# Half of a depthwise convolution moved from TensorE to VectorE and ScalarE, with new scheduler durations and dummy matmuls, in a pooled-attention and gated feed-forward kernel

## Chip, cores, metric

One NeuronCore of a Trainium2 chip. The metric is the device time of one execution in microseconds, the median of a kernel's runs; the profile of an execution shows a span that is 1.7 to 2.4 us shorter than its time. Engines are named as in the profile: PE (TensorE), PEld (its weight loads), DVE (VectorE), ACT (ScalarE), POOL (GpSimd), SP (SyncE).

## The reference

```python
# q, k, v: (8, 8, 576, 64) fp32;  w_in (512, 1024), conv_w (3, 1024), w_out (1024, 512)
k_p = k.reshape(B, H, 72, 8, D).mean(axis=3)              # pool k and v over 8 positions
v_p = v.reshape(B, H, 72, 8, D).mean(axis=3)
attn = softmax(q @ k_p.T / sqrt(D));  x = attn @ v_p      # x: (8, 576, 512) after the heads are joined
h = relu(x @ w_in)                                        # (8, 576, 1024)
conv_out[s] = conv_w[0] * h[s-1] + conv_w[1] * h[s] + conv_w[2] * h[s+1]   # per feature, zero padded
out = (h * sigmoid(conv_out)) @ w_out                     # (8, 576, 512)
```

The convolution has three taps for each feature. With features on partitions and positions along the free dimension it is either three matmuls with diagonal weights that accumulate in PSUM, or three multiplies by a per-partition scalar and two adds.

## The kernel before

The kernel writes each operation as a task with an estimated duration, the buffers it reads and writes, and a priority. A list scheduler (`Planner`) simulates the engines with these estimates and emits the instructions of each engine in that order. The estimates cost no time themselves: they decide the order, and every engine then works through its own list in that order.

```python
class Planner:
    N_PS = 4                 # PSUM slots, each a tile of [P, 2, 512] in fp32
    DMA_RATE = 220e3         # bytes per us that the planner assumes for loads
    DMA_LAT = 2.2
    SEM = 0.12
    LAT = {"PE": 0.20, "ACT": 0.16, "DVE": 0.10, "POOL": 0.12, ...}
    # ... order(): takes the operation that can start first, by priority, on the engine that ends it first

def conv(b, f, pr):                                   # batch b, block f of 128 features
    def fn(e):
        t = slot(key)
        for kk in range(3):
            for i in range(2):
                nc.tensor.matmul(out=t[:, i, 0:HC], lhsT=dw[:, f, kk, :],       # diagonal weights
                                 rhs=hT[m][:, f, 1 + kk + i * HC:1 + kk + (i + 1) * HC],
                                 start=(kk == 0), stop=(kk == 2))
    pl.add(f"conv.{b}.{f}", "PE", 0.73, fn, ...)
    # ScalarE: tg = tanh(conv / 2) from PSUM;  VectorE: tg += 1;  VectorE: gT = tg * hT
# ... mm1: h block (8 matmuls), relu on ScalarE into hT;  mm2: 128 rows of the output (8 matmuls of 512)
```

One batch runs through loads, sums over k and v (DVE), transposes (PE) with evacuations (ACT or DVE), scores (PE), exponentials (ACT), the product with v (PE), normalisation (DVE), transposes and copies, then `mm1`, the convolution, the gate and, for two batches at a time, `mm2`. The planner interleaves the attention of batch b+1 with the feed-forward of batch b.

The softmax here doesn't subtract the row's maximum and nothing guards it: scores larger than these inputs give would overflow.

## Time and profile before

| | before |
|---|---|
| time, median of 3 runs first (262.15 to 262.91) | 262.34 us |
| span of the profiled run | 259.9 us |
| busy: PE / DVE / ACT | 235.1 / 126.8 / 166.5 us |
| first product block of batch 0 starts | 23.3 us |
| first product block of batch 1 starts | 62.0 us |
| last product block ends | 244.2 us |

The last three rows are milestones in the trace that divide the run into a prologue (attention alone), the first batch's feed-forward with the hole in which batch 1's attention stands almost alone, a dense part with PE close to full, and a tail. The prediction below shows the lines that carry this.

### The profile page before, as it was taken

The page shows a single profiled execution, that of the slowest core. Times are in us where ns is not written, and L with a number is a line of the kernel's source. Part 1 is how long each engine was busy: PE and PEld are TensorE (multiplying, and loading weights), DVE is VectorE, ACT ScalarE, POOL GpSimd, SP SyncE. Part 2 cuts the span into 40 slices and gives each one's busy share as a digit, 9 for nine tenths or more (in the row PEclk, how much of TensorE's full clock was granted, in tenths as well). Part 3 has the DMA queues.
Part 4 walks back from the last instruction along what each step waited for, and adds up shares of the span by engine and source line. Part 5 has one row for each costly group of instructions (what it writes and reads, how often), then busy time and mean ns, then how long its engine had stood idle before and what let it go on. Part 6 is the DMA issues. An engine that isn't in the chain of part 4 may idle for free.

```text
span 259.9 us, 4786 instructions
## 1 busy us (share of the span) xinstructions
PE 235.1 (90%) x1985; PEld 166.9 (64%) x1985; DVE 126.8 (49%) x307; ACT 166.5 (64%) x271; POOL 25.6 (10%) x47
## 2 busy tenths in 40 slices
PE   0488997969999999999999999999999999999992
PEld 0356774458877767676757767686768767667540
DVE  2684346556587628923766427421753237123210
ACT  1574673657978857686658856596658855547521
POOL 8761001302102101210000000000000000000000
PEclk9995999968999999999999999999999999999999
DMA  7999997996854774894207002020102102102214
GB/s 180 204 199 208 207 205 113 195 201 114 130 89 83 105 127 112 143 171 108 82 0 171 23 21 83 0 83 32 49 6 78 43 0 83 57 25 83 81 40 161
DMA packets 20617, 26.60 MB, mean 102 GB/s; under 512 B 2396, under 2 KB 14516, under 8 KB 20596
## 3 DMA queue, kind: packets, MB, share of 16 engines
q0 software_dynamic: 15024, 15.67, 38.5%
q1 hardware_dynamic: 5572, 10.63, 11.8%
q8 instruction: 15, 0.25, 0.4%
q14 instruction: 6, 0.05, 0.1%
HBM read 32.52 MB, written 9.44 MB: 161 GB/s over the span
## 4 chain that ended last, share of the span: by engine, by line
PE 76%; ACT 13%; DVE 6%; DMA 3%; issue 1%; ACTq 0%; POOLq 0%
PE psf L478 24%; PE psf L531 23%; PE psf L497 18%; PE psf L402 5%; ACT tg L504 3%; DMA q_b<-in_q_dram 3%; ACT attnT L413 3%; DVE xx L443 2%; PE psb L385 2%; ACT osb L539 2%; PE psb L457 2%; PE psf L430 1%; ACT xT L463 1%; ACT qT L391 1%; ACT kTz L357 1%
## 5 line engine op out<-in xcount | busy, mean ns | idle before, releaser
L478 PE MATMUL psf<-xT,w_in 128*128 128x288 bf16 x512 | 74.4, 290 | 1.2 <-ACT xT L463 0.5
L531 PE MATMUL psf<-w_out,gT 128*128 128x512 bf16 x288 | 65.9, 379 | 1.4 <-DVE gT L514 1.1
L509 DVE TENSOR_SCALAR tg<-tg 128x576 bf16<-128x576 bf16 x64 | 20.1, 314 | 82.9 <-ACT tg L504 82.3
L478 PEld LDWEIGHTS <-w_in 128*128 128x128 bf16 x512 | 50.3, 99 | 15.7 <-issue 1.5
L497 PE MATMUL psf<-hT,dw 128*128 128x288 bf16 x384 | 57.9, 286 | 1.1 <-ACT kTz L357 1.0
L484 ACT ACTIVATE hT<-psf 128x576 bf16<-128x576 f32 x64 | 41.7, 652 | 18.0 <-PE psf L478 17.6
L531 PEld LDWEIGHTS <-gT 128*128 128x128 bf16 x288 | 27.9, 98 | 32.0 <-DVE gT L514 2.2
L504 ACT ACTIVATE tg<-psf 128x576 bf16<-128x576 f32 x64 | 41.5, 649 | 7.7 <-PE psf L497 2.4
L539 ACT COPY osb<-psf 128x1024 f32<-128x1024 f32 (+1 forms) x20 | 18.5, 927 | 42.3 <-PE psf L531 42.3
L497 PEld LDWEIGHTS <-dw 128*128 128x128 bf16 x384 | 37.1, 97 | 11.2 <-issue 1.8
L413 ACT ACTIVATE attnT<-psf 72x576 bf16<-72x576 f32 x64 | 39.7, 644 | 1.9 <-PE psf L402 1.9
L514 DVE TENSOR_TENSOR gT<-tg,hT 128x576 bf16<-128x576 bf16 x64 | 29.0, 453 | 1.5
L402 PE MATMUL psf<-qT,kTz 128*72 128x288 bf16 x128 | 26.0, 303 | 2.2 <-ACT qT L391 1.4
L443 DVE TENSOR_TENSOR xx<-psf,rr 128x512 bf16<-128x512 f32 x40 | 26.8, 684 | 0.4
L385 PE MATMUL psb<-ident,q_b 128*128 128x128 bf16 x144 | 12.9, 240 | 9.2 <-DMA q_b<-in_q_dram 8.5
L402 PEld LDWEIGHTS <-kTz 128*72 128x72 bf16 x128 | 15.4, 120 | 6.8 <-issue 1.6
L430 PE MATMUL psf<-vaug,attnT 72*128 72x65 bf16 x320 | 16.3, 198 | 2.5 <-ACT attnT L413 1.1
L391 ACT COPY qT<-psb 128x768 bf16<-128x768 bf16 x17 | 13.1, 805 | 8.5 <-PE psb L385 8.5
L457 PE MATMUL psb<-perm,xx 128*128 128x128 bf16 x160 | 16.9, 237 | 1.5 <-DVE xx L443 1.1
L430 PEld LDWEIGHTS <-attnT 72*128 72x128 bf16 x320 | 14.3, 101 | 5.2 <-ACT attnT L413 3.0
L463 ACT COPY xT<-psb 128x512 bf16<-128x512 bf16 (+1 forms) x25 | 13.2, 536 | 6.8 <-PE psb L457 6.6
L385 PEld LDWEIGHTS <-q_b 128*128 128x128 bf16 x144 | 10.6, 109 | 10.3 <-DMA q_b<-in_q_dram 8.6
(39 smaller groups left out, 115.5 us busy)
## 6 DMA issues: line engine op xcount, KB each, us to landing
out_dram<-osb SPq DMA_DIRECT2D x16, 512.0 KB, 2.8
v_b<-in_v_dram POOLq DMA_DIRECT2D x8, 576.0 KB, 11.3
k_b<-in_k_dram POOLq DMA_DIRECT2D x7, 576.0 KB, 7.6
q_b<-in_q_dram POOLq DMA_DIRECT2D x7, 576.0 KB, 6.4
k_f<-in_k_dram SPq DMA_DIRECT2D x2, 576.0 KB, 5.8
w_in<-in_moe_w_in_dram POOLq DMA_DIRECT2D x4, 256.0 KB, 10.2
w_out<-in_moe_w_out_dram POOLq DMA_DIRECT2D x2, 512.0 KB, 13.8
out_dram<-osb SPq DMA_DIRECT2D x4, 256.0 KB, 2.0
```

The source lines that it names most:

```text
L385: nc.tensor.transpose(out=t[:, 0, i * P:(i + 1) * P], in_=q_b[m][:, j:j + 2, :].rearrange("p i d -> p (i d)"), identity=ident)
L402: nc.tensor.matmul(out=t[0:Sp, par, 0:HC], lhsT=kTz[m][:, par, h * Sp:(h + 1) * Sp], rhs=qT[m][:, :, h * A:(h + 1) * A], start=True, stop= ...
L413: nc.scalar.activation(out=attnT[m][:, h, :].rearrange("p (c i x) -> p i c x", i=2, x=32), in_=slot(key)[0:Sp, :, 0:HC].rearrange("p i (c ...
L430: nc.tensor.matmul(out=a[:, h // 4, c:c + D + 1], lhsT=attnT[m][:, h, u0:u0 + 128], rhs=vaug[m][:, h, :], start=True, stop=True)
L443: nc.vector.tensor_tensor(out=xx[i3].rearrange("p (g h e) -> p g h e", g=2, h=4), in0=av_view()[:, :, :, 0:D], in1=rr[i3].rearrange("p (g ...
L478: nc.tensor.matmul(out=t[:, i, 0:HC], lhsT=w_in[:, c, f * P:(f + 1) * P], rhs=xT[m][:, c, i * HC:(i + 1) * HC], start=(c == 0), stop=(c == ...
L484: nc.scalar.activation(out=hT[m][:, f, 2:S + 2].rearrange("p (i x) -> p i x", i=2), in_=slot(key)[:, :, 0:HC], func=ACT.Relu, scale=0.5)
L497: nc.tensor.matmul(out=t[:, i, 0:HC], lhsT=dw[:, f, kk, :], rhs=hT[m][:, f, 1 + kk + i * HC:1 + kk + (i + 1) * HC], start=(kk == 0), stop= ...
L504: nc.scalar.activation(out=tg[i3].rearrange("p (i x) -> p i x", i=2), in_=slot(key)[:, :, 0:HC], func=ACT.Tanh, scale=0.5)
L514: nc.vector.tensor_tensor(out=gT[(b // 2) % 2][:, f, o:o + S], in0=tg[i3], in1=hT[m][:, f, 2:S + 2], op=OP.mult)
L531: nc.tensor.matmul(out=a[:, x, :], lhsT=g[:, c, t * P:(t + 1) * P], rhs=w_out[:, c, :], start=(c == 0), stop=(c == n_fb - 1))
L539: copy_on(e)(out=osb[i3][:, 0:n, :], in_=slot(key)[:, 0:n, :])
```

## The change

The intent: take work from PE, the bound. Convolution blocks 1, 3, 5 and 7 of each batch go to VectorE and ScalarE in bf16; the planner gets durations and latencies nearer to the trace, and a higher load rate; dummy matmuls on a zeroed tile fill planned PE gaps of the first 24 us, to keep the array's clock up; and each PSUM tile takes the slot that the planner gave it. Cut to its core:

```diff
-    DMA_RATE = 220e3
-    DMA_LAT = 2.2
-    SEM = 0.12
+    DMA_RATE = 330e3
+    DMA_LAT = 2.0
+    SEM = 0.05
+    WARM = 24.0
...
+            if e == "PE" and s < self.WARM and s - free.get(e, 0.0) > 0.3:
+                ...   # a free slot x:  self.gaps[i] = (s - f0, x)
...
+    def warm(gap, x):
+        t = pp.tile([P, 2, 512], FP32, name="psw", tag=f"ps{x}")
+        for _ in range(min(int((gap - 0.2) / 0.1), 60)):
+            nc.tensor.matmul(out=t[:, 0, 0:P], lhsT=zero[:, 0:P], rhs=zero[:, 0:P], start=True, stop=True)
...
+    OFF = [(1, 3, 5, 7) for b in range(B)]
...
+    def conv_off(b, f, pr):
+        for kk in (1, 0, 2):
+            def fn(e, kk=kk):
+                s = cw[:, kk * n_fb + f:kk * n_fb + f + 1]
+                src = hT[m][:, f, 1 + kk:1 + kk + S]
+                if e == "ACT":
+                    nc.scalar.activation(out=cv[y][:, kk, :], in_=src, func=ACT.Copy, scale=s)
+                else:
+                    nc.vector.tensor_scalar(out=cv[y][:, kk, :], in0=src, scalar1=s, scalar2=None, op0=OP.mult)
+            pl.add(f"cp{kk}.{b}.{f}", {"DVE": 0.225, "ACT": 0.59}, 0, fn, ...)
+        for kk in (0, 2):
+            def fn(e, kk=kk):
+                nc.vector.tensor_tensor(out=cv[y][:, 1, :], in0=cv[y][:, 1, :], in1=cv[y][:, kk, :], op=OP.add)
+            pl.add(f"ca{kk}.{b}.{f}", "DVE", 0.375, fn, ...)
+        # then tanh on ScalarE, from SBUF
...
-            pl.add(f"qTe.{b}.{g}", {"ACT": 0.73, "DVE": 0.95}, 0, fn, ...)
+            pl.add(f"qTe.{b}.{g}", {"ACT": 0.71, "DVE": 0.475}, 0, fn, ...)
         # ... some twenty other durations in the same way; kz on DVE 0.72 -> 0.375, xte on DVE 0.66 -> 0.345
```

More of the change, by code (lines that the diff above doesn't have):

```diff
@@ L61, in add @@
         return o.i
-    LAT = {"PE": 0.20, "ACT": 0.16, "DVE": 0.10, "POOL": 0.12, "SP": 0.0, "ACTQ": 0.0}
+    LAT = {"PE": 0.17, "ACT": 0.10, "DVE": 0.08, "POOL": 0.12, "SP": 0.0, "ACTQ": 0.0}
     def order(self):
@@ L73, in order @@
         free = {}
-        slots = [0.0] * self.N_PS
-        held = {}
+        slots = {i: 0.0 for i in range(self.N_PS)}
+        held = self.held = {}
+        live = set()
+        self.gaps = {}
         dma_free = 0.0
@@ L87, in order @@
                         continue
-                    st = max(st, min(slots))
+                    st = max(st, min(slots.values()))
                 cand = None
@@ L106, in order @@
             if o.take is not None and o.take not in held:
-                slots.remove(min(slots))
-                held[o.take] = True
+                x = min(slots, key=lambda y: (slots[y], y))
+                del slots[x]
+                held[o.take] = x
+            if e == "PE" and s < self.WARM and s - free.get(e, 0.0) > 0.3:
+                f0 = max(free.get(e, 0.0), 0.6)
+                x = min(slots, key=lambda y: (slots[y], y)) if slots else None
+                if x is not None and slots[x] <= f0 and s - f0 > 0.3:
+                    self.gaps[i] = (s - f0, x)
             free[e] = s + d
@@ L116, in order @@
             if o.give is not None:
-                del held[o.give]
-                slots.append(o.done)
+                slots[held[o.give]] = o.done
             out.append((s, e, d, o))
@@ L157 @@
     sb = ctx.enter_context(tc.tile_pool(name="sb", bufs=1))
-    pp = ctx.enter_context(tc.tile_pool(name="pp", bufs=4, space=bass.MemoryType.PSUM))
+    pp = ctx.enter_context(tc.tile_pool(name="pp", bufs=1, space=bass.MemoryType.PSUM))
     def st(name, shape, dt):
@@ L163 @@
     ident = st("ident", [P, P], BF16)
+    zero = st("zero", [P, P], BF16)
     identf = st("identf", [24, 24], FP32)
@@ L188 @@
     hT = [st(f"hT{i}", [P, n_fb, S + 4], BF16) for i in range(2)]
+    cv = [st(f"cv{i}", [P, 3, S], BF16) for i in range(2)]
     tg = [st(f"tg{i}", [P, S], BF16) for i in range(3)]
@@ L197, in slot @@
         if key not in ps:
+            tag = f"ps{pl.held[key]}"
             if bf:
-                ps[key] = pp.tile([P, 2, 1024], BF16, name="psb", tag="ps")
+                ps[key] = pp.tile([P, 2, 1024], BF16, name="psb", tag=tag)
             else:
-                ps[key] = pp.tile([P, 2, 512], FP32, name="psf", tag="ps")
+                ps[key] = pp.tile([P, 2, 512], FP32, name="psf", tag=tag)
         return ps[key]
+    def warm(gap, x):
+        t = pp.tile([P, 2, 512], FP32, name="psw", tag=f"ps{x}")
+        for _ in range(min(int((gap - 0.2) / 0.1), 60)):
+            nc.tensor.matmul(out=t[:, 0, 0:P], lhsT=zero[:, 0:P], rhs=zero[:, 0:P], start=True, stop=True)
     def copy_on(e):
@@ L267, in fn @@
         def fn(e):
+            nc.vector.memset(zero, 0.0)
+        zi = pl.add("zero", "DVE", 0.15, fn, writes=["zero"], prio=-80)
+        def fn(e):
             make_identity(nc, ident)
@@ L325, in fn @@
                     nc.vector.tensor_tensor(out=kp1[:, c, :], in0=k_f[:, c, 0:256], in1=k_f[:, c, 256:512], op=OP.add)
-                pl.add(f"kp1.{b}.{i}", "DVE", 0.9, fn, reads=[("kf", i)], writes=[("kp1", i)], prio=pr)
+                pl.add(f"kp1.{b}.{i}", "DVE", 0.875, fn, reads=[("kf", i)], writes=[("kp1", i)], prio=pr)
         else:
@@ L329, in fn @@
                 nc.vector.tensor_tensor(out=kp1, in0=k_b[m][:, :, 0:256], in1=k_b[m][:, :, 256:512], op=OP.add)
-            pl.add(f"kp1.{b}", "DVE", 0.9, fn, reads=[("k", m)], writes=[("kp1", 0), ("kp1", 1)], prio=pr)
+            pl.add(f"kp1.{b}", "DVE", 0.875, fn, reads=[("k", m)], writes=[("kp1", 0), ("kp1", 1)], prio=pr)
         def fn(e):
             nc.vector.tensor_tensor(out=kp2, in0=kp1[:, :, 0:128], in1=kp1[:, :, 128:256], op=OP.add)
-        pl.add(f"kp2.{b}", "DVE", 0.5, fn, reads=[("kp1", 0), ("kp1", 1)], writes=["kp2"], prio=pr)
+        pl.add(f"kp2.{b}", "DVE", 0.475, fn, reads=[("kp1", 0), ("kp1", 1)], writes=["kp2"], prio=pr)
         def fn(e):
@@ L343, in fn @@
             )
-        pl.add(f"ksum.{b}", "DVE", 0.5, fn, reads=["kp2"], writes=["ksum"], prio=pr)
+        pl.add(f"ksum.{b}", "DVE", 0.475, fn, reads=["kp2"], writes=["ksum"], prio=pr)
         key = ("kT", b)
@@ L352, in fn @@
                                     in_=ksum[:, i].rearrange("p i d -> p (i d)"), identity=ident[0:KR, 0:KR])
-        pl.add(f"kT.{b}", "PE", 0.30, fn, reads=["ksum", "ident"], writes=[("kTp", b)], prio=pr, take=key)
+        pl.add(f"kT.{b}", "PE", 0.35, fn, reads=["ksum", "ident"], writes=[("kTp", b)], prio=pr, take=key)
         for h in range(2):
@@ L357, in fn @@
                 copy_on(e)(out=kTz[m][c, h, :], in_=slot(key)[c, 0, 0:H * Sp])
-            pl.add(f"kz.{b}.{h}", {"DVE": 0.72, "ACT": 0.57}, 0, fn, reads=[("kTp", b), ("kz", m)], writes=[("kTz", m, h)], prio=pr,
+            pl.add(f"kz.{b}.{h}", {"DVE": 0.375, "ACT": 0.55}, 0, fn, reads=[("kTp", b), ("kz", m)], writes=[("kTz", m, h)], prio=pr,
                    give=key if h == 1 else None)
@@ L365, in fn @@
             nc.vector.tensor_tensor(out=vp1, in0=v_b[m][:, :, 0:256], in1=v_b[m][:, :, 256:512], op=OP.add)
-        pl.add(f"vp1.{b}", "DVE", 1.15, fn, reads=[("v", m)], writes=["vp1"], prio=pr)
+        pl.add(f"vp1.{b}", "DVE", 1.14, fn, reads=[("v", m)], writes=["vp1"], prio=pr)
         def fn(e):
             nc.vector.tensor_tensor(out=vp2, in0=vp1[:, :, 0:128], in1=vp1[:, :, 128:256], op=OP.add)
-        pl.add(f"vp2.{b}", "DVE", 0.62, fn, reads=["vp1"], writes=["vp2"], prio=pr)
+        pl.add(f"vp2.{b}", "DVE", 0.61, fn, reads=["vp1"], writes=["vp2"], prio=pr)
         def fn(e):
             nc.vector.tensor_tensor(out=vaug[m][:, :, 0:D], in0=vp2[:, :, 0:D], in1=vp2[:, :, D:2 * D], op=OP.add)
-        pl.add(f"va.{b}", "DVE", 0.36, fn, reads=["vp2", ("v8", m)], writes=[("va", m)], prio=pr)
+        pl.add(f"va.{b}", "DVE", 0.34, fn, reads=["vp2", ("v8", m)], writes=[("va", m)], prio=pr)
     def attn_q(b, pr):
@@ L386, in fn @@
                                         in_=q_b[m][:, j:j + 2, :].rearrange("p i d -> p (i d)"), identity=ident)
-            pl.add(f"qT.{b}.{g}", "PE", 0.36, fn, reads=[("q", m, g), "ident"], writes=[("qTp", b, g)],
+            pl.add(f"qT.{b}.{g}", "PE", 0.40, fn, reads=[("q", m, g), "ident"], writes=[("qTp", b, g)],
                    prio=pr[g], take=key)
@@ L391, in fn @@
                 copy_on(e)(out=qT[m][:, 6 * g:6 * g + 6, :], in_=slot(key)[:, 0, 0:768].rearrange("p (j c) -> p j c", c=P))
-            pl.add(f"qTe.{b}.{g}", {"ACT": 0.73, "DVE": 0.95}, 0, fn, reads=[("qTp", b, g)], writes=[("qT", m, g)],
+            pl.add(f"qTe.{b}.{g}", {"ACT": 0.71, "DVE": 0.475}, 0, fn, reads=[("qTp", b, g)], writes=[("qT", m, g)],
                    prio=pr[g], give=key)
@@ L417, in fn @@
             )
-        pl.add(f"exp.{b}.{h}", "ACT", 0.58, fn, reads=[("scp", b, h)], writes=[("at", m, h)], prio=pr, give=key)
+        pl.add(f"exp.{b}.{h}", "ACT", 0.55, fn, reads=[("scp", b, h)], writes=[("at", m, h)], prio=pr, give=key)
     def attn_av(b, t, pr):
@@ L431, in fn @@
                                  rhs=vaug[m][:, h, :], start=True, stop=True)
-        pl.add(f"av.{b}.{t}", "PE", 0.32, fn, reads=[("at", m, h) for h in range(H)] + [("va", m)],
+        pl.add(f"av.{b}.{t}", "PE", 0.36, fn, reads=[("at", m, h) for h in range(H)] + [("va", m)],
                writes=[("avp", b, t)], prio=pr, take=key)
@@ L439, in fn @@
             nc.vector.reciprocal(out=rr[i3].rearrange("p (g h) -> p g h", g=2), in_=av_view()[:, :, :, D])
-        pl.add(f"rc.{b}.{t}", "DVE", 0.16, fn, reads=[("avp", b, t)], writes=[("rr", i3)], prio=pr)
+        pl.add(f"rc.{b}.{t}", "DVE", 0.13, fn, reads=[("avp", b, t)], writes=[("rr", i3)], prio=pr)
         def fn(e):
@@ L448, in fn @@
             )
-        pl.add(f"nm.{b}.{t}", "DVE", 0.64, fn, reads=[("avp", b, t), ("rr", i3)], writes=[("xx", i3)], prio=pr, give=key)
+        pl.add(f"nm.{b}.{t}", "DVE", 0.61, fn, reads=[("avp", b, t), ("rr", i3)], writes=[("xx", i3)], prio=pr, give=key)
         key2 = ("xt", b, t)
@@ L466, in fn @@
             )
-        pl.add(f"xte.{b}.{t}", {"ACT": 0.52, "DVE": 0.66}, 0, fn, reads=[("xtp", b, t)], writes=[("xT", m, t)],
+        pl.add(f"xte.{b}.{t}", {"ACT": 0.49, "DVE": 0.345} if not last else {"ACT": 0.28, "DVE": 0.21}, 0, fn, reads=[("xtp", b, t)], writes=[("xT", m, t)],
                prio=pr + 0.3, give=key2)
@@ L479, in fn @@
                                      rhs=xT[m][:, c, i * HC:(i + 1) * HC], start=(c == 0), stop=(c == n_dc - 1))
-        pl.add(f"mm1.{b}.{f}", "PE", 0.97, fn, reads=[("xT", m, t) for t in range(n_t)] + [("wi", f // 2)],
+        pl.add(f"mm1.{b}.{f}", "PE", 0.98, fn, reads=[("xT", m, t) for t in range(n_t)] + [("wi", f // 2)],
                writes=[("hp", b, f)], prio=pr, take=key)
@@ L485, in fn, with conv_pe @@
                                  in_=slot(key)[:, :, 0:HC], func=ACT.Relu, scale=0.5)
-        pl.add(f"relu.{b}.{f}", "ACT", 0.58, fn, reads=[("hp", b, f)], writes=[("hT", m, f)], prio=pr, give=key)
-    def conv(b, f, pr):
+        pl.add(f"relu.{b}.{f}", "ACT", 0.55, fn, reads=[("hp", b, f)], writes=[("hT", m, f)], prio=pr, give=key)
+    n_off = [0]
+    def conv_off(b, f, pr):
+        m = b % 2
+        i3 = (b * n_fb + f) % 3
+        y = n_off[0] % 2
+        n_off[0] += 1
+        for kk in (1, 0, 2):
[6 more added lines that the diff above has]
+                    nc.vector.tensor_scalar(out=cv[y][:, kk, :], in0=src, scalar1=s, scalar2=None, op0=OP.mult)
+            pl.add(f"cp{kk}.{b}.{f}", {"DVE": 0.225, "ACT": 0.59}, 0, fn, reads=[("hT", m, f), ("hz", m), "cw"],
+                   writes=[("cv", y, kk)], prio=pr)
+        for kk in (0, 2):
+            def fn(e, kk=kk):
+                nc.vector.tensor_tensor(out=cv[y][:, 1, :], in0=cv[y][:, 1, :], in1=cv[y][:, kk, :], op=OP.add)
+            pl.add(f"ca{kk}.{b}.{f}", "DVE", 0.375, fn, reads=[("cv", y, 1), ("cv", y, kk)], writes=[("cv", y, 1)], prio=pr)
+        def fn(e):
+            nc.scalar.activation(out=tg[i3], in_=cv[y][:, 1, :], func=ACT.Tanh, scale=0.5)
+        pl.add(f"tanh.{b}.{f}", "ACT", 0.59, fn, reads=[("cv", y, 1)], writes=[("tg", i3)], prio=pr)
+    def conv(b, f, pr):
+        m = b % 2
+        i3 = (b * n_fb + f) % 3
+        if f in OFF[b]:
+            conv_off(b, f, pr)
+        else:
+            conv_pe(b, f, pr)
+        def fn(e):
+            nc.vector.tensor_scalar(out=tg[i3], in0=tg[i3], scalar1=1.0, scalar2=None, op0=OP.add)
+        pl.add(f"tg1.{b}.{f}", "DVE", 0.225, fn, reads=[("tg", i3)], writes=[("tg", i3)], prio=pr)
+        def fn(e):
+            o = (b % 2) * S
+            nc.vector.tensor_tensor(out=gT[(b // 2) % 2][:, f, o:o + S], in0=tg[i3], in1=hT[m][:, f, 2:S + 2], op=OP.mult)
+        pl.add(f"g.{b}.{f}", "DVE", 0.375, fn, reads=[("tg", i3), ("hT", m, f)], writes=[("gT", (b // 2) % 2, f, b % 2)],
+               prio=pr)
+    def conv_pe(b, f, pr):
         m = b % 2
@@ L499, in fn @@
                                      start=(kk == 0), stop=(kk == 2))
-        pl.add(f"conv.{b}.{f}", "PE", 0.73, fn, reads=[("hT", m, f), ("hz", m)] + [("dw", f, kk) for kk in range(3)],
+        pl.add(f"conv.{b}.{f}", "PE", 0.745, fn, reads=[("hT", m, f), ("hz", m)] + [("dw", f, kk) for kk in range(3)],
                writes=[("cp", b, f)], prio=pr, take=key)
@@ L505, in fn @@
                                  func=ACT.Tanh, scale=0.5)
-        pl.add(f"tanh.{b}.{f}", "ACT", 0.58, fn, reads=[("cp", b, f)], writes=[("tg", i3)], prio=pr, give=key)
-        def fn(e):
-            nc.vector.tensor_scalar(out=tg[i3], in0=tg[i3], scalar1=1.0, scalar2=None, op0=OP.add)
-        pl.add(f"tg1.{b}.{f}", "DVE", 0.27, fn, reads=[("tg", i3)], writes=[("tg", i3)], prio=pr)
-        def fn(e):
-            o = (b % 2) * S
-            nc.vector.tensor_tensor(out=gT[(b // 2) % 2][:, f, o:o + S], in0=tg[i3], in1=hT[m][:, f, 2:S + 2], op=OP.mult)
-        pl.add(f"g.{b}.{f}", "DVE", 0.42, fn, reads=[("tg", i3), ("hT", m, f)], writes=[("gT", (b // 2) % 2, f, b % 2)],
-               prio=pr)
+        pl.add(f"tanh.{b}.{f}", "ACT", 0.55, fn, reads=[("cp", b, f)], writes=[("tg", i3)], prio=pr, give=key)
     n_o = [0]
@@ L539, in fn @@
             copy_on(e)(out=osb[i3][:, 0:n, :], in_=slot(key)[:, 0:n, :])
-        pl.add(f"oe.{pair}.{tiles[0]}", {"ACT": 0.09 + 0.43 * n, "DVE": 0.09 + 0.535 * n}, 0, fn,
+        pl.add(f"oe.{pair}.{tiles[0]}", {"ACT": 0.066 + 0.427 * n, "DVE": 0.075 + 0.535 * n}, 0, fn,
                reads=[("op", pair, t) for t in tiles], writes=[("osb", i3)], prio=pr, give=key)
@@ L588 @@
         for s, e, d, o in pl.order():
+            if o.i in pl.gaps:
+                warm(*pl.gaps[o.i])
             o.fn(e)
```

## The prediction

> **What bounds the kernel now.** I read the page first, parts 1, 2 and 4 (engine totals, slices, shares of the chain that ended last).
>
> ```profile
> PE 235.1 (90%) x1985; PEld 166.9 (64%) x1985; DVE 126.8 (49%) x307; ACT 166.5 (64%) x271; POOL 25.6 (10%) x47
> ...
> PE   0488997969999999999999999999999999999992
> ...
> PEclk9995999968999999999999999999999999999999
> ...
> PE 76%; ACT 13%; DVE 6%; DMA 3%; issue 1%; ACTq 0%; POOLq 0%
> ```
>
> TensorE is busy in every slice but the first and last few, and it is three quarters of the chain. [...]I read the chain piece by piece (start, length, what), here from the middle of the first batch's feed-forward:
>
> ```profile
> 30.52 0.74 PE psf L497 x6
> 31.26 0.98 PE psf L478 x8
> 32.24 0.74 PE psf L497 x6
> 32.99 0.98 PE psf L478 x8
> ```
>
> One convolution block (L497, 6 matmuls of 288 columns) follows one block of the first product (L478, 8 matmuls) without a gap: 0.74 us is 123 ns per matmul. So a block of the convolution is worth its full 0.74 us on the chain wherever PE is the bound. Where that is so the table of stretches tells (length, then busy us of PE, PEld, DVE, ACT, POOL, granted clock, DMA share, GB/s):
>
> ```profile
> 8.00:23.00 15.00, 11.34 (x101) 8.60 (x102) 12.26 (x37) 10.90 (x22) 8.15 (x17) 0.90 1.31 202
> ...
> 38.20:62.00 23.80, 19.39 (x165) 13.13 (x165) 14.26 (x30) 13.22 (x21) 3.45 (x5) 0.86 0.92 160
> ...
> 120.00:160.00 40.00, 39.01 (x355) 28.24 (x354) 22.43 (x54) 26.79 (x44) 0.58 (x1) 1.00 0.23 64
> ```
>
> From 80 to 240 us the four 40 us stretches have PE busy 39.4, 39.0, 39.0 and 39.8 us: 157 of 160. The two stretches above are the holes. In 8 to 23 us the first batch's attention runs alone, and in 38 to 62 us the second batch's attention runs with only four tiles of the last product to fill it. The chain there stands on ScalarE and VectorE, and the matmuls are slow: in 20 to 26 us those of L478 took 443 ns each against 285 ns in 100 to 140 us, where the record has the clock at 0.50 and 1.00. The tail:
>
> ```profile
> 246.15 0.66 ACT tg L504
> ...
> 246.83 0.32 DVE tg L509
> ...
> 247.18 0.47 DVE gT L514
> ...
> 247.69 7.31 PE psf L531 x33
> ...
> 255.07 1.01 ACT osb L539
> ```
>
> After the last convolution PE has little left to do until tanh, the +1 and the gate have run. Last, the groups that the change touches or copies in kind:
>
> ```profile
> L509 DVE TENSOR_SCALAR tg<-tg 128x576 bf16<-128x576 bf16 x64 | 20.1, 314 | 82.9 <-ACT tg L504 82.3
> ...
> L497 PE MATMUL psf<-hT,dw 128*128 128x288 bf16 x384 | 57.9, 286 | 1.1 <-ACT kTz L357 1.0
> ...
> L504 ACT ACTIVATE tg<-psf 128x576 bf16<-128x576 f32 x64 | 41.5, 649 | 7.7 <-PE psf L497 2.4
> ...
> L514 DVE TENSOR_TENSOR gT<-tg,hT 128x576 bf16<-128x576 bf16 x64 | 29.0, 453 | 1.5
> ```
>
> L509 and L514 are the same operations, shape and type as the new multiplies and adds, so their durations price them. VectorE waits 82 us for ScalarE before L509: it has room.
>
> [...] the rows differ by 453 - 314 = 139 ns. [...] In the list by form the five weight scalings on ScalarE (L301, 128 elements, the same kind of operand) take 395 ns [...], and eight exponentials of 644 ns end in 4.28 us, 535 ns apart: an overlap of 109. [...] cold from about 19 us, L478 starts at 23.32, and the clock is back at about 26.7.
>
> **The change, part by part.** *Convolution.* Four of eight blocks in each of eight batches leave PE: 32 x 0.74 = 23.7 us. The counts of the built program confirm it: 192 matmuls of that line instead of 384. In their place come 96 multiplies and 64 adds; the order gives 76 multiplies to VectorE and 20 to ScalarE. One after the other, a VectorE operation costs about 85 ns less than its duration (two of L443, 684 ns each, took 1.24 us). So VectorE gets 76 x 0.23 + 64 x 0.37 = 41 us. The new durations also move evacuations from ScalarE to it: xT 15 to 27, qT 7 to 13, kTz 5 to 9, which at (422, 554, 454) - 85 ns is 4.0 + 2.8 + 1.5 = 8 us. Durations in the list by form sum to some 135 us before, 110 us after the overlap is taken off, so VectorE goes to about 159 us. [...] PE, by the same spacing (64 x 0.98 first product, 36 x 1.73 last product, 64 x 0.74 convolution, about 52 us of attention), goes from 224 to about 201 us. PE stays the largest by 40 us: all 23.7 us should come off the path, less what new waits give back.
>
> *New durations in the planner.* They set the order only. With loads assumed at 330 instead of 220 GB/s (of fp32 read) the second batch's attention now stands directly behind the eight product blocks of batch 0, and the four fill tiles of the last product move on into the dense part. Does the data come in time? In the trace the second q landed 21.7 us after its issue at 14.38, at 36.1; the second v 23.5 us after 15.52, at 39.0. PE reaches that q at 23 + 8 x 0.98 + 4 x 0.74 + about 2 (cold clock) = 36 us: just in time. From there I price the hole on the first batch's pattern: transposes and evacuation 2.3 us, eight exponentials 4.3 us, five tiles of normalisation, transposes and copies 5.3 us (18.01 to 23.32 before) and about 1.5 us for other VectorE work in between. The product of batch 1 starts at about 49.5 us, and PE has done some 9 us of work in those 13.5: idle 4.5 to 5. Before, 23.8 us held 4 x 1.73 plus about 9, that is 16 us at spacing: idle 7.7. Gain 2.8 us.
>
> *Dummy matmuls.* 84 of them: 47 before the first transpose, 23, 3, 7 and 4 later. The first 47 take 47 x 0.107 = 5 us at half clock, hidden behind the load that lands at 8.46. The 23 may delay the second transposes by 1.3 us (55 ns each); the transposes after them save 70 to 100 ns each. But the prologue's chain is the load, then evacuations, then exponentials paced by ScalarE, then VectorE, where PE's clock counts for little. Between 13 and 23 us hardly any dummies stand, so I expect the clock to fall again and the first product to start cold as before. Gain 0.5 us, which could be zero.
>
> *What is given back.* A moved block needs relu, three multiplies, two adds, tanh, +1 and gate: about 4.3 us from the product's end instead of some 2.7. In the dense part VectorE's load rises from 50% to 66%, and it also feeds ScalarE (tanh), whose queue frees PSUM. I let PE's idle share there go from 1.8% to 4.5% over 155 us: +4.2 us, a choice. At the end block 7 is a moved one, and only one convolution (0.74) and seven matmuls (1.5) cover its 4.3 us chain, against a wait of about 1.1 us before: +1.0 us.
>
> Sum: 262.3 - 23.7 - 2.8 - 0.5 + 4.2 + 1.0 = 240.5; I say 241.
>
> **The rivals.** *A: VectorE and ScalarE become the bound*, through the longer chain: tanh waits in ScalarE's queue for VectorE's adds, relu behind it frees PSUM late (four slots), and PE stalls. For it: five engine changes per moved block, [...]. Against it: a batch is 25 us of PE but only 20 of VectorE [...]. PE's idle would rise to 10%: 249 us. *B: the waits stay as small as before* and the second hole closes more: 1.8% idle, tail unchanged, which gives 262.3 - 23.7 - 2.8 - 0.5 = 235. *C: the loads are late.* If PE, in order, stands before transposes whose q comes later than planned, in the second and third batch, the hole reopens by 4 to 6 us: 246. 330 GB/s is above what I get from the landings (about 11.3 MB of fp32 read by 39 us: some 300). *D: the clock.* If PE, now idle 10%, falls to half clock once per batch, each costs about 1.7 us: 253. Nothing after 62 us speaks for it.
>
> **Range and chances.** B and a mild C span 234 to 247; I take 234 to 248. Slower than 257 (the 2% line) needs A and D together. Faster 0.95, same 0.04, slower 0.01.
>
> **What would show it.** Right: PE's convolution group at 192 matmuls of the same duration; VectorE busy near 175 to 180 us and ScalarE near 165, both below PE's; multiplies near 315 ns for all three taps and adds near 453 ns; batch 1's first product at 48 to 51 us; PE idle in the dense part around 4%; a first product still cold at 24 us. Wrong: [...] PE waits headed by tanh or relu that wait for VectorE adds (A); waits on the q loads between 34 and 48 us (C); a clock of 0.5 after 60 us (D); a first product that runs at full clock, which would make the dummies worth about 1.7 us more.

Cut where marked is what no trace or run of this case shows, with what rested on it: rates per cycle, alignment, the price of a per-partition scalar on ScalarE (and with it ScalarE's total of 153 us and its share of a batch), and when the clock rises. No term of the sum is cut: 262.3 - 23.7 - 2.8 - 0.5 + 4.2 + 1.0 came to 240.5. ScalarE "near 165" stands as forecast, without its derivation. "The same kind of operand" is a per-partition scalar, as in the new multiplies.

Some prices are estimates, and the trace of the kernel before has these numbers for them. The 85 ns per VectorE operation: single L443 stand in the chain with 0.60 to 0.61 us, 74 to 84 ns under their 684; the pair named, 1.24 us, is 128 ns under twice 684. The 55 ns of a dummy: what 123 ns for 288 columns scales to at 128 (1.45 us for the 23, 63 ns each, in the changed kernel). The 70 to 100 ns that a transpose saves: one of q took 310 ns from 8 to 13 us and 219 from 100 to 140 us, one of k 278 and 206. A cold first product: the first 24 matmuls of L478 took 4.73 us against 3 x 0.98, 1.8 us more (the "about 2"), and half of the time from 23.32 to 26.7 us is 1.7.

## The result

| | before | after |
|---|---|---|
| time, median (range; 4 runs each) | 262.25 us (262.11 to 262.91) | 245.37 us (244.63 to 246.63) |
| span of the profiled run | 259.9 | 243.0 |
| busy PE / DVE / ACT | 235.1 / 126.8 / 166.5 | 217.2 / 174.1 / 165.5 |

The ratio is 0.9357 (95% interval 0.9308 to 0.9405). Ratios here are the mean time of one kernel's fast runs over the mean of the other's of the same rounds, so not quite the ratio of the medians.

The page of the changed kernel, engine totals, slices and shares of the chain:

```profile
PE 217.2 (89%) x1877; PEld 153.1 (63%) x1877; DVE 174.1 (72%) x470; ACT 165.5 (68%) x269; POOL 26.5 (11%) x47
...
PE   8566996589979999899999999999999999999691
...
DVE  2597399989699997995499657933987659447500
...
PEclk9996799959999999999999999999999999999999
...
PE 56%; DVE 19%; ACT 19%; DMA 3%; issue 1%; ACTq 0%; DVEq 0%; POOLq 0%
```

PE is still the busiest, but its share of the chain fell from 76% to 56%, and VectorE's rose from 6% to 19%. The PE row shows where PE is not full: slices 2 to 4 (6 to 24 us, at 6.1 us a slice) and 7 and 8 (36 to 49 us) are at 5 or 6 tenths, slice 12 is at 7 and slice 38, near the end, at 6; but for the last slice the rest are at 8 or 9.

The groups of the page that the prediction priced, now line by line of the changed kernel (busy us, mean ns | idle before):

```profile
L524 DVE TENSOR_SCALAR cv<-hT,cw 128x576 bf16<-128x576 bf16 x76 | 24.2, 367 | 28.4 <-ACT hT L506 28.2
...
L563 PE MATMUL psf<-hT,dw 128*128 128x288 bf16 x192 | 29.0, 286 | 0.0
L529 DVE TENSOR_TENSOR cv<-cv 128x576 bf16<-128x576 bf16 x64 | 28.5, 445 | 0.4
...
L545 DVE TENSOR_SCALAR tg<-tg 128x576 bf16<-128x576 bf16 x64 | 19.5, 304 | 11.7 <-ACT tg L533 11.7
```

The convolution on PE is halved at the same 286 ns. The adds take 445 ns (priced from 453). The multiplies take 367 ns, 63 more than the +1 of L545, which has the same shape and type but an immediate in place of the per-partition scalar. In this trace 73 of the 76 lie between 356 and 373 ns (the others are 321, 322 and 502 ns); at least 44 of the 76 are of the two outer taps, which start 2 bytes off a 4-byte boundary.

The milestones, from the starts of the first-product matmuls in the two traces (a block ends one spacing after the start of its last matmul), make the ledger. In the new order four tiles of the last product (4 x 1.73 = 6.9 us) stand behind the second milestone, so I count them where they stood before:

| stage | before | after | change, those tiles set right | predicted |
|---|---|---|---|---|
| prologue, to the first product of batch 0 | 23.3 | 25.4 | +2.1 | -0.5 |
| to the first product of batch 1 | 38.6 | 29.3 | -2.4 | -3.0 - 2.8 = -5.8 |
| to the end of the last product block | 182.3 | 171.6 | -17.6 | -20.0 + 4.2 = -15.8 |
| tail, to the end | 15.7 | 16.7 | +1.0 | -0.7 + 1.0 = +0.3 |
| sum | 259.9 | 243.0 | -16.9 | -21.8 |

The predicted column splits the 32 blocks of 0.74 us by stage: four in the first batch, 27 in the dense part, the last one in the tail. The first two rows fall short by 6.0 us and the tail by 0.7; the dense part gained 1.8 more than predicted, so that 4.9 us are missing in all.

**Prologue.** The chain of work in order of time (start, length, what), before:

```profile
10.25 0.66 PE psb L351 x6
...
12.16 0.68 ACT qT L391
12.84 0.89 ACT dw L301 x3
13.73 4.28 ACT attnT L413 x8
```

and after:

```profile
8.50 0.52 PE psb L407 x6
...
9.05 0.56 DVE qT L413
9.61 0.87 DVE kp L347
...
13.40 1.28 ACT dw L323 x4
...
14.70 4.42 ACT attnT L435 x8
```

The planner now finds VectorE cheap for evacuations (0.475) and puts that of the first q transposes (L413) ahead of the second half of the sum over k (L347). That half ran at 8.04 us before; now it stands behind an evacuation that waits for the q load, and starts at 9.52. Four weight scalings on ScalarE (L323) then stand ahead of the exponentials.

**The hole.** The chain of the changed kernel from 33 to 47.7 us is VectorE alone:

```profile
33.68 0.87 DVE kp L351
...
36.22 0.56 DVE cv L524 x2
37.01 0.37 DVE cv L529
...
38.73 1.49 DVE qT L413 x3
...
41.17 1.13 DVE vp L387
...
44.76 0.88 DVE kp L351
...
46.41 1.26 DVE xx L465 x2
```

Convolution multiplies and adds (L524, L529), k sums, q evacuations and v sums of batch 1, and even the k sum of batch 2 (the second L351) stand in one queue ahead of the normalisation (L465) that the first product of batch 1 waits for. The table of stretches for 34 to 48 us has VectorE busy 13.8 of 14 us and PE 9.6. Nothing on PE or VectorE waits for a load between 30 and 55 us.

From 47.7 us on the chain changes between VectorE and transposes on PE, of batch 2 as well as of batch 1, and the clock records have PE at half speed from 47.6 to 54.5 us:

```profile
48.99 0.65 PE psb L373 x6
...
50.84 1.45 PE psb L407 x12
...
53.53 0.61 PE psb L479 x4
```

The six k transposes (L373) take 0.65 us here and 0.43 in experiment 5, which has no half-clock stretch in its hole. So the hole has a second part, the clock, which no run separates from VectorE's queue.

### The profile page after: what moved, and what is told of

It is laid out like the page before. It is cut to its first block, busy times and chain, and to the rows that moved or that the text cites. A ratio compares the mean times of both kernels' runs of the same rounds, so it can differ in the third digit from the quotient of the medians.

```text
span 243.0 us, 4692 instructions
## 1 busy us (share of the span) xinstructions
PE 217.2 (89%) x1877; PEld 153.1 (63%) x1877; DVE 174.1 (72%) x470; ACT 165.5 (68%) x269; POOL 26.5 (11%) x47
## 4 chain that ended last, share of the span: by engine, by line
PE 56%; DVE 19%; ACT 19%; DMA 3%; issue 1%; ACTq 0%; DVEq 0%; POOLq 0%
PE psf L587 25%; PE psf L500 17%; ACT hT L506 5%; PE psf L563 4%; ACT attnT L435 4%; PE psf L424 4%; DVE xx L465 3%; DMA q_b<-in_q_dram 3%; PE psb L479 3%; ACT osb L595 3%; DVE cv L524 2%; DVE cv L529 2%; PE psb L407 2%; ACT cv L522 2%; ACT tg L533 2%; ACT tg L570 2%
## 5 line engine op out<-in xcount | busy, mean ns | idle before, releaser
L500 PE MATMUL psf<-xT,w_in 128*128 128x288 bf16 x512 | 72.3, 288 | 0.7
L524 DVE TENSOR_SCALAR cv<-hT,cw 128x576 bf16<-128x576 bf16 x76 | 24.2, 367 | 28.4 <-ACT hT L506 28.2
L435 ACT ACTIVATE attnT<-psf 72x576 bf16<-72x576 f32 x64 | 39.9, 652 | 0.6 <-PE psf L424 0.5
L533 ACT ACTIVATE tg<-cv 128x576 bf16<-128x576 bf16 x32 | 21.8, 687 | 11.8 <-DVE cv L529 11.7
L563 PE MATMUL psf<-hT,dw 128*128 128x288 bf16 x192 | 29.0, 286 | 0.0
L529 DVE TENSOR_TENSOR cv<-cv 128x576 bf16<-128x576 bf16 x64 | 28.5, 445 | 0.4
L424 PE MATMUL psf<-qT,kTz 128*72 128x288 bf16 x128 | 24.8, 287 | 3.6 <-DVE qT L413 1.9
L545 DVE TENSOR_SCALAR tg<-tg 128x576 bf16<-128x576 bf16 x64 | 19.5, 304 | 11.7 <-ACT tg L533 11.7
L465 DVE TENSOR_TENSOR xx<-psf,rr 128x512 bf16<-128x512 f32 x40 | 27.1, 684 | 0.2
L479 PE MATMUL psb<-perm,xx 128*128 128x128 bf16 x160 | 17.6, 240 | 5.3 <-DVE xx L465 4.7
L570 ACT ACTIVATE tg<-psf 128x576 bf16<-128x576 f32 x32 | 20.7, 646 | 0.8
L563 PEld LDWEIGHTS <-dw 128*128 128x128 bf16 x192 | 18.2, 97 | 4.5
L424 PEld LDWEIGHTS <-kTz 128*72 128x72 bf16 x128 | 14.4, 114 | 8.3 <-issue 4.7
L479 PEld LDWEIGHTS <-xx 128*128 128x128 bf16 x160 | 11.9, 106 | 10.3 <-DVE xx L465 8.0
```

Of the source, the lines that this page charges most:

```text
L424: nc.tensor.matmul(out=t[0:Sp, par, 0:HC], lhsT=kTz[m][:, par, h * Sp:(h + 1) * Sp], rhs=qT[m][:, :, h * A:(h + 1) * A], start=True, stop= ...
L435: nc.scalar.activation(out=attnT[m][:, h, :].rearrange("p (c i x) -> p i c x", i=2, x=32), in_=slot(key)[0:Sp, :, 0:HC].rearrange("p i (c ...
L465: nc.vector.tensor_tensor(out=xx[i3].rearrange("p (g h e) -> p g h e", g=2, h=4), in0=av_view()[:, :, :, 0:D], in1=rr[i3].rearrange("p (g ...
L479: nc.tensor.transpose(out=a[:, 0, c * P:(c + 1) * P], in_=xx[i3][:, c * P:(c + 1) * P], identity=perm)
L500: nc.tensor.matmul(out=t[:, i, 0:HC], lhsT=w_in[:, c, f * P:(f + 1) * P], rhs=xT[m][:, c, i * HC:(i + 1) * HC], start=(c == 0), stop=(c == ...
L524: nc.vector.tensor_scalar(out=cv[y][:, kk, :], in0=src, scalar1=s, scalar2=None, op0=OP.mult)
```

## The experiments

Kernels of one group ran on one chip; the runs of the kernel before stand beside each group (262.40, 261.91 and 261.86 us). "First exponential" is the first L435 (L413 in the kernel before).

**1 to 3: the parts of the change, one at a time.**

Without the dummies:

```diff
-            if e == "PE" and s < self.WARM and s - free.get(e, 0.0) > 0.3:
+            if False and e == "PE" and s < self.WARM and s - free.get(e, 0.0) > 0.3:
```

> The changed kernel without its 84 dummy matmuls, nothing else. My theory (the prologue's chain runs over VectorE and ScalarE, and PE's clock falls again before the first product): no effect, 245.4 us within 1 us, exponentials start near 14.7 us, the first product at 25.4 us and still cold. Rival H (the 23 dummies delay the second group of transposes by 1.5 us and thereby the chain): 243.9 us, first product at 24 us. Rival W (the dummies warm the array and pay): 247 us, first product later or slower than 2.96 us for its first 16 matmuls by 1 us.

Measured: 246.1 us (245.7 to 246.9), ratio 0.9394; first exponential at 15.05 us, first product at 25.50. Against 245.37 and 0.9357 with them the medians differ by 0.7 us, and the intervals overlap. The dummies have no effect that these runs resolve.

The new durations alone (with the slots that belong to them):

```diff
+            if False and e == "PE" and s < self.WARM and ...
-    OFF = [(1, 3, 5, 7) for b in range(B)]
+    OFF = [() for b in range(B)]
```

> The new planner constants alone: all convolutions on PE, no dummies. My theory (the new order gains little: it moves four tiles of the last product out of the second hole, and the prologue is 2 us later): 258 to 263 us against 262.3 of before. The second hole should be shorter than in the changed kernel, since VectorE has 12 convolution multiplies and 8 adds less in it: first product of the second batch at most 54.7 + 3.0 - 3 us. Rival (the new order is worth as much as the planner hopes, some 10 us or more): 252 us or less.

Measured: 257.7 us (257.4 to 258.7), ratio 0.984. The order alone is worth 4.2 us by the ratio and 4.7 by the medians, a little more than the 258 to 263 that I expected, far from the rival's 10. In its trace the first product of batch 1 starts at 54.4 us, no later than with half of the first batch's convolution taken off PE (54.7; 55.9 in the run without dummies). Its clock records have no half-clock stretch in the hole, which may be part of this. So the four moved blocks of the first batch gained nothing on the way to that point.

The moved convolution alone, with the old constants, grafted into the kernel before (its durations in the old style: multiplies 0.27 and 0.62, adds 0.42, tanh 0.62):

```diff
     # the kernel before, and:
+    cv = [st(f"cv{i}", [P, 3, S], BF16) for i in range(2)]
+    OFF = [(1, 3, 5, 7) for b in range(B)]
+    def conv_off(b, f, pr): ...      # as in the change
```

> The moved convolution alone: the old planner constants and PSUM rotation, with four of eight blocks on VectorE and ScalarE, no dummies. My theory (PE bounds all but prologue, second hole and tail; the removed 23.7 us come off less 2.2 us of new waits in the dense part and 1.9 us at the tail; prologue as before): 262.3 - 23.7 + 4.1 = 242.7 us, with 3 us more if the old order suits the longer chain worse: 242 to 247. Rival (the old order cannot use the room, VectorE waits in the dense part): 250 us or more.

Measured: 250.8 us (250.6 to 251.3), ratio 0.9572. That is 11.6 us of the 23.7 taken from PE, and my expectation of 242 to 247 was wrong; the rival's number was right. But the loss is not in the dense part, as the rival had it: between the first product of batch 1 and the end of the last product block this kernel needs 166.4 us, against 182.3 before, 15.9 of 20.0. The rest went in the hole. Its first product of batch 1 starts at 65.3 us, 3.3 us *later* than before. The timeline of PE in that run (start, length, group, idle before and its releaser) shows why:

```profile
35.72 0.66 PE L544 MATMUL psf<-hT,dw 128*128 128x288 bf16 x4
41.93 0.66 PE L354 MATMUL psb<-ident,ksum 96*128 96x96 bf16 x6 [5.55 <-DVE ksum L341]
```

PE finishes the first batch's convolution earlier and then sits idle for 5.55 us until VectorE has got through gates, multiplies and adds to the sum over k. The k transposes start no later than before (41.93 us against 42.18). But before, PE had done one tile of the last product ahead of them; here all four stand behind them, and the first ran at the half clock that the records have from 41.4 to 44.9 us. The q transposes come at 47.06 us, not 44.17. In the total the two parts of the change nearly add: 11.6 us for the convolution alone and 4.7 for the order alone, against 17.0 together, a difference within the noise. It is in the hole that they need each other: with the convolution alone that stage is 3.5 us longer, with both 2.4 us shorter (tiles set right).

**4: the tail.**

```diff
-    OFF = [(1, 3, 5, 7) for b in range(B)]
+    OFF = [(1, 3, 5, 7)] * 7 + [(1, 3, 5)]
```

> The changed kernel with block 7 of the last batch back on PE (31 moved blocks, not 32). My theory (the moved chain of the last block is exposed: PE idles 2.2 us between its last product and the last 33 matmuls): that idle time falls to about 0.3 us, PE gets 0.74 us of convolution back, so 1.2 us less: 244.2 us. Rival (the tail is set by the copies of the last product out of PSUM, not by the last gate): no change, 245.4 us.

Measured: 245.7 us (244.7 to 247.2), ratio 0.9376: no gain in the total. In the trace, though, the stage from the end of the last product block to the end took 15.7 us against 16.7, and the last 33 matmuls started 3.5 us after that block's end against 4.4. What hides it is probably the clock. The four runs at mean clocks of 0.945, 0.951, 0.940 and 0.972 took 246.0, 245.3, 247.2 and 244.7 us; those of the changed kernel at 0.970, 0.971, 0.951 and 0.953 took 244.7, 244.6, 246.6 and 246.0. In these eight runs clock and time go together, and PE's half-clock stretches come in lengths of 3.4, 6.8 and 10.2 us in the clock records: in this run they were 3.4 + 10.2 + 10.2 us before the dense part, in the profiled run of the changed kernel 6.8 + 6.8. So the mechanism is seen in the stage, and the gain of 1 us in the total is not shown by these runs. That the clock is what hides it is argued from these eight runs and two traces, not tested. Other kernels here don't follow the mean clock so plainly: experiment 11 took 236.87 us both at 0.974 and at 0.952, and the fastest run of experiment 10, 234.24 us, had 0.975 where three at 0.983 took 235.2 to 236.0.

**5: is PE the bound in the first batch?**

```diff
+    OFF = [()] + [(1, 3, 5, 7)] * 7
```

> The changed kernel with the convolution of the first batch back on PE (28 moved blocks). My theory (in the first batch PE is not the bound: VectorE is full from 34 to 48 us and sets when the second batch's product can start): the 3.0 us that PE gets back cost nothing, the second batch's first product stands at 54.7 us within 1 us or earlier, total 244 to 246 us. Rival (PE bounds the first batch too, as the prediction had it): first product of the second batch and the end 3 us later, 248.4 us.

Measured: 244.0 us (243.2 to 244.9), ratio 0.9318; the first product of batch 1 starts at 53.8 us, 1.0 us earlier than in the changed kernel though PE has 3.0 us more to do before it. Four traces with the changed order in this stretch (the changed kernel, experiments 1, 4 and 8) have it at 54.7 to 56.3. The rival's 248.4 is ruled out: PE's work in the first batch does not set the time. That VectorE's queue does is what the chain above shows, up to 47.7 us. For the stretches 34 to 48 us (us, then busy PE, PEld, DVE, ACT, POOL) the changed kernel has

```profile
34.00:48.00 14.00, 9.64 (x106) 7.09 (x104) 13.78 (x33) 11.71 (x20) 2.87 (x4) 0.99 1.20 200
```

and this one

```profile
34.00:48.00 14.00, 12.81 (x129) 9.85 (x128) 11.59 (x24) 10.96 (x19) 2.88 (x4) 1.00 1.16 191
```

PE's idle 4.4 us of those 14 became 1.2, and VectorE got room. The records of this run have PE at full clock from 28.8 to 230 us, so a part of what it gained in the hole can be the clock. In its tail they have a stretch of 3.4 us at half clock, as in experiments 6 and 7: the tails of these three took 18.3 us, against 16.7 in the changed kernel, which hides 1.7 us of whatever the edits gained.

**6 and 7: what delays the prologue?** First only the twelve weight tiles that nothing reads any more are left out; then the order is mended as well.

```diff
-        for f in range(n_fb):
+        for f in [x for x in range(n_fb) if any(x not in o for o in OFF)]:     # both
-                pl.add(f"dw{f}.{kk}", {"ACT": 0.3, "DVE": 0.2}, ...)            # the second kernel, from here on
+                pl.add(f"dw{f}.{kk}", {"DVE": 0.21}, ...)
-            pl.add(f"qTe.{b}.{g}", {"ACT": 0.71, "DVE": 0.475}, ...)
+            pl.add(f"qTe.{b}.{g}", {"ACT": 0.71} if b == 0 and g == 0 else {"ACT": 0.71, "DVE": 0.475}, ...)
-            pl.add(f"kz.{b}.{h}", ..., reads=[("kTp", b), ("kz", m)], ...)
+            pl.add(f"kz.{b}.{h}", ..., reads=[("kTp", b), ("kz", m)] + ([("kTz", m, 0)] if h else []), ...)
```

> The changed kernel without the 12 diagonal weight tiles of the moved blocks, which nothing reads. My theory (the scalings on ScalarE between the second evacuation and the first exponential, 13.4 to 14.7 us, lie on the chain): if the planner still leaves scalings there, no change; each one taken from there brings the exponentials and all after them 0.3 us forward, 1.2 us at most: 244.2 to 245.4 us. Rival (they run in idle time): 245.4 us and the first exponential still at 14.7 us.

Measured: 246.4 us (245.5 to 247.7), ratio 0.9412; first exponential at 14.60 us against 14.70. No gain. But the planner left four scalings (L323, 1.28 us) in this run's chain just ahead of the first exponential, so the run does not test what they cost.

> The changed kernel with the prologue mended: the first evacuation of q for the first batch on ScalarE, not VectorE, so that the sum over k need not wait behind it for the q load; scalings of the weights on VectorE only, and only those in use; the planner knows that the two halves of the k copy run one after the other. My theory (the prologue lost 2.1 us because VectorE's order put the q evacuation ahead of the second k sum, and because four scalings stand before the exponentials): sum over k at 8.1 us in place of 9.6, first exponential at 13.2 us in place of 14.7, first product at 24 us, total 243.9 us. Rival (the dummies between the first two groups of transposes set it): first exponential stays at 14.7 us and the total at 245.4.

Measured: 245.2 us (242.1 to 245.7), ratio 0.9323; the second half of the sum over k ran at 7.94 us as intended, yet the first exponential came at 14.38 us and the first product at 25.1. My account of the prologue was incomplete. The chain of this run:

```profile
8.37 0.51 PE psb L407 x6
8.88 2.37 PE psw L220 x23
11.25 0.64 PE psb L407 x6
```

With VectorE out of the way, the 23 dummies (L220) are on the chain: 2.37 us, 103 ns each, at half clock. After the first 47 dummies PE had been idle for 2.5 us until the load came, and the clock records have it at half speed from 8.8 us for 3.4. The rival was right that the dummies delay the transposes. In the trace of the changed kernel they ran at full clock, 1.45 us, and VectorE's order took as long at the same place and hid them. In experiment 4, with the same prologue but the clock down from 8.6 us, the same 23 took 2.45 us, stood on the chain, and the first exponential came at 15.40 us: one order, two chains, depending on when the clock fell.

**8: how far does the dense part follow PE?**

```diff
+    OFF = [(1, 3, 5, 7)] + [(0, 2, 4, 6, 7)] * 6 + [(1, 3, 5, 7)]
```

> The changed kernel with five of eight blocks moved in batches 1 to 6 (38 blocks, not 32). My theory (the dense part is bound by PE, with 1.3 us of each pair's 5.9 given back): 6 x 0.74 us less, of which a fifth to a third is given back: 241.9 to 242.4 us. Rival A (VectorE and ScalarE are at their limit there): no gain or a loss, 245 us or more, with PE waits on product copies or gates.

Measured: 241.9 us (240.3 to 242.7), ratio 0.9228, as expected. From the first product of batch 1 to the end of the last block: 167.6 us against 171.6, 4.0 of the 4.4 us taken from PE. At four blocks VectorE and ScalarE are not at their limit in the dense part.

**9 to 11: the repairs together.** The ninth kernel is the seventh without dummies.

> The mended prologue without the dummy matmuls. In the mended prologue with dummies, the 23 dummies between the first two groups of transposes took 2.37 us at half clock and stood on the chain in VectorE's place. My theory now (two delays of nearly the same length ran side by side: VectorE's order and the dummies; each alone hides the other): with both gone the first exponential starts at 12.9 us within 0.4 us in place of 14.4 to 15.0, the first product at 23.7 us, total about 243.5 us [...]. Rival (the chain ahead of the exponentials has a third cause, the cold transposes, which the dummies had kept fast): first exponential not before 14 us.

Measured: first exponential at 12.98 us, first product at 23.8; 244.4 us (244.3 to 245.0), ratio 0.9342. Both delays are confirmed as causes: either alone holds the exponentials at 14.4 us or later, and with both gone they start 1.7 us earlier than in the changed kernel (14.70 to 15.40 us in the four traces with its prologue: its own and experiments 4, 5 and 8). The mended order is a bundle, though: the evacuation and the scalings both left the way. In the traces the last copy of the k transposes (kTz) ends at 12.17 us, not 13.38, and the exponentials follow it after 0.8 us, not 1.3; no run separates the parts. The q transposes now run at half clock (311 ns each, 219 in the changed kernel; in the kernel before they took 301 ns from 55 to 61 us, at a mean recorded clock of 0.52), so the rival's third cause is ruled out. A recorded 1.00 early in a run does not prove full clock: here it stands from 22 to 30 us, though the first 14 matmuls of the first product took 441 ns each; in the kernel before they took 285 ns at 1.00 (100 to 140 us). The total is 1.0 us lower, with intervals that overlap.

> A version meant to beat both: mended prologue, no dummies, measured durations for the new multiplies in the planner (0.31 us on VectorE, 0.68 us on ScalarE), two of eight blocks moved in the first batch, five in batches 1 to 6, three (not the last one) in the last batch. My theory (the gains of the single edits add: 1.5 us in the prologue, 3.5 us in the dense part, 1 us at the tail, 0.5 us in the first batch): 239.5 us, 238 to 241. Rival (VectorE, then near 180 us, takes back what PE gives): 242 us or more.

```diff
     # the ninth kernel, and:
+    OFF = [(1, 3)] + [(0, 2, 4, 6, 7)] * 6 + [(1, 3, 5)]
-            pl.add(f"cp{kk}.{b}.{f}", {"DVE": 0.225, "ACT": 0.59}, ...)
+            pl.add(f"cp{kk}.{b}.{f}", {"DVE": 0.31, "ACT": 0.68}, ...)
```

Measured: **236.0 us** (234.2 to 236.6, 6 runs), ratio 0.9005 (0.8977 to 0.9033): 9.4 us faster than the changed kernel and below my 238 to 241. Its page:

```profile
PE 210.2 (90%) x1758; PEld 147.3 (63%) x1775; DVE 180.5 (77%) x487; ACT 165.7 (71%) x267; POOL 25.6 (11%) x47
...
PE   0587999799979999999999999899999999999991
```

The dip at the end of the PE row is gone (slice 38 is 9, not 6), and of the dip in slices 7 and 8 one slice at 7 is left. It gained more than I expected. Its dense part takes 164.6 us with 33 moved blocks there, against 171.6 with 27: six blocks explain 4.4 us, and 1.7 us is one tile of the last product that this order runs before the milestone. The 0.9 us left is no more than this stage differs between kernels with the same 27 blocks (170.9 to 172.0 us in experiments 5, 7 and 9). The corrected multiply durations are the one edit not tested alone; what they are worth stays open.

> The same with six of eight blocks moved in batches 1 to 6. My theory (VectorE is now about as full as PE in the dense part, some 22 of 24 us for a batch, so a sixth block gives back what it takes): within 1 us of the version with five. Rival A (PE is still the bound): 4.4 us less, a third given back, 3 us faster. Rival B (VectorE is over its limit): 2 us slower or more.

```diff
+    OFF = [(1, 3)] + [(0, 1, 2, 4, 5, 6)] * 6 + [(1, 3, 5)]
```

Measured: 236.5 us (234.4 to 236.9), ratio 0.9017 (0.8981 to 0.9053): the same as with five. In its dense part PE waits 2.0 us for normalisations and 1.8 us for xT copies on VectorE, and the clock records have one half-clock stretch of 3.4 us at 120 us. The sixth block gained nothing that these runs show; they cannot say how much of that is the clock.

## Why the prediction was right, and where it was not

The time, 245.4 us, lies in the range of 234 to 248, and it is faster by over 2% as forecast. By its own steps:

- **The removed work, "all 23.7 us should come off the path, less what new waits give back": right in the dense part, wrong in the first batch.** Against the kernel with the new order alone, which needs 186.9 us from the first product of batch 1 to the end of the last block, the changed kernel needs 171.6: 15.3 of 20.0 us arrive, 4.7 are given back. I had chosen 4.2, and that it came so close is partly luck: PE's recorded idle time in the stage grew only from 2.6 to 5.2 us, 3.0% where I had chosen 4.5, and where the other 2.1 us went stays open. The longest wait there is not rival A's (tanh or relu) but PE's for VectorE's normalisations, 1.7 us from 80 to 205 us. (Against the kernel before the stage gained 17.6, because the order brings 2.3 there too, which I had not counted. Without them the time would have been 247.7 us, at the very edge of the range: that they made up for a part of the misses is luck as well.) In the first batch 3.0 us came off PE and nothing off the path: experiments 2 and 5.
- **"Gain 2.8 us" in the second hole: failed.** I priced the hole on the first batch's pattern with "about 1.5 us for other VectorE work in between". In the trace VectorE has 13.8 us of work in the 14 us from 34 to 48, with the multiplies and adds of the first batch, and the sum over the next batch's k, ahead of the normalisation. The first product of batch 1 stands at 54.7 us, not 49.5 or the 48 to 51 that I gave as the sign of being right. About two of the 5.2 us are the late prologue; the rest is VectorE's queue and, from 47.7 us on, transposes at half clock, in shares that no run separates. The queue is rival A, at a place where I had not looked for it: I compared VectorE's total with PE's and not its work between these two points.
- **"Gain 0.5 us" in the prologue: failed; it lost 2.1 us.** I had taken the chain from the kernel before and not walked it through the new order: VectorE's list has the q evacuation before the second half of the sum over k, so that a sum that was ready at 8 us waits for a load. My other thought, that the 23 dummies "may delay the second transposes", was right: they took 1.45 us in the trace of the changed kernel, hidden behind VectorE's order, and 2.4 us on the chain where the clock was at half (experiments 4 and 7).
- **Dummies: right.** The first 47 took 5.20 us in the changed kernel, 106 ns from start to start (0.107 us in the prediction; the 23 took 103 ns each in experiment 7 at a recorded half clock), and PE was idle for 2.3 us after them until the load came. The clock fell again before the first product (records: half clock from 20.3 to 27.2 us; I had read the earlier fall in the kernel before as "about 19 us", its record has 19.9), as predicted, and they are worth nothing that can be measured.
- **Tail: the size.** I gave 1.0 us for the longer chain of the last block, a wait of 4.3 - 0.74 - 1.5 = 2.1 us against "about 1.1 us before". The chain did take 4.3 us (226.49 to 230.77), and the wait 1.9:

```profile
PE psf L587 <- DVE gT L550: 1.9, 2, 1.0
```

The wrong term is the old wait. In the kernel before PE has no gap longer than 0.13 us between its last first-product block and the last 33 matmuls, because the convolutions of two blocks (1.66 us) and seven matmuls of the last product fill that time. So the wait grew by 1.7 us, not 1.0; with the 0.7 us of convolution that left, the tail lost 1.0, and experiment 4 gets that back.

- **Unit prices.** Adds 445 ns (453 predicted), multiplies on VectorE 367 ns where I had 314: the 53 ns that I had not priced make about 4 us of VectorE in all. The per-partition scalar is the likely reason (the +1 of the same trace, with an immediate, takes 304 ns); the +1 also works in place, which no run tests. ScalarE multiplies took 770 ns. VectorE is busy 174.1 us (175 to 180 predicted) and ScalarE 165.5 (165). Whether the start off a 4-byte boundary costs anything was not tested: no run holds the kernel fixed and shifts only the start. With at least 44 such multiplies among the 76, 73 took 356 to 373 ns.
- **Rivals B, C and D.** B did not happen in this kernel. C did not: nothing waits for a load in the hole. D did not in the dense part; but PE fell to half clock in the prologue and the hole (records: 20.3 to 27.2 and 47.6 to 54.5 us), and the four runs of the changed kernel are slower where their mean clock is lower (244.6 us at 0.971, 246.6 at 0.951). The 0.8% between these two is more than the difference between its median and that of six of the seven kernels of experiments 1 and 4 to 9.

## What to carry to other kernels

When work moves from the bound engine to others, compare the loads stretch by stretch, not over the run: a total of 72% can be 98% just where the bound engine waits, and moved work was worth nothing there. After a scheduler's prices change, walk the first chain through the new order of *every* engine; an operation that waits for a load and stands ahead of one that is ready can cost the whole wait (here a sum that ran at 8.04 us before started at 9.52). And when one repair shows nothing, look at what took its place on the chain: here two delays of nearly equal length lay side by side, and only removing both showed either.
